# Making float32 weights from double-precision words: VectorE's last three steps replaced by one rounding pass and an integer add on GpSimd

## Chip, core and metric

The kernel runs on one core of a Trainium2 chip. The metric is the device time of one execution in microseconds. Times shown are medians over runs of the same kernel.

The engines are named as in the profile: PE is TensorE, DVE is VectorE, ACT is ScalarE, POOL is GpSimd, and SP is SyncE, which only issues DMAs here. PEld is PE's loading of stationary operands.

## What is computed

A recurrence over 768 time steps (RWKV-7) for 4 batches of 8 heads with head dimension 40, and after it an MLP with a sigmoid-gated activation on the 3072 rows of 320 channels that come out.

```python
state = zeros((B, H, D, D))
for t in range(S):
    y[:, :, t] = einsum('bhd,bhde->bhe', r_t, state)
    Sa = einsum('bhde,bhe->bhd', state, a_t)
    state = state * w_t[:, :, None, :] - einsum('bhd,bhe->bhde', Sa, b_t)
    state = state + einsum('bhd,bhe->bhde', v_t, k_t)
x = y.transpose(0, 2, 1, 3).reshape(B * S, H * D)
h = x @ w_in                                   # 320 -> 2048
out = (h * (1 / (1 + exp(-1.702 * h)))) @ w_out  # 2048 -> 320
```

The two weight matrices arrive as 64-bit floating-point numbers. The kernel works in float32, so it has to turn each 64-bit number into a 32-bit one on the chip.

## The kernel before

**The recurrence in chunks.** The 768 steps are cut into 12 chunks of 64, and the batches into two pairs, so there are 24 units; unit `i` is chunk `i // 2`, pair `i % 2`. Within a unit the steps are solved together by matmuls on PE: sums of logarithms of the decay (`ps_cum`, `ps_cumc`), scores (`ps_N`, `ps_A`, `ps_RV`), the inverse of a triangular matrix in five levels (`ps_level`, then `ps_Q`, `ps_T`), and then the part that depends on the state of the chunk before (`zr`, `ps_zT`, `ps_rz`, `ps_B`, `ps_X`, `ps_y`). Only this last part runs in order from chunk to chunk. Between the matmuls DVE, ACT and POOL copy, mask and scale: L686 and L665 are DVE's transposes between two levels, L747 and L714 copies of a level's result, L787 and L861 DVE's steps before `ps_X` and `ps_y`, L583, L588 and L591 scalings on POOL or DVE, L907 the scaling of the output `x`. L545 to L556 on ACT are the exponentials of a unit (L542 loads their table), L492 and L493 the logarithms for a later unit.

**The MLP.** When both pairs of a chunk are through, `x` goes to DRAM and comes back transposed (L917, L921), and the MLP of the chunk runs: four groups of 40 matmuls `ps_up` (L275 is the helper that issues every matmul), each followed by the gated activation on ACT (L942), and two groups of 64 matmuls `ps_down`, which add up over all four activations, with a copy (L966), an add (L968) and a store. Four pairs of PSUM banks are shared by all matmul groups. The MLP's matmuls are also what PE does while the recurrence waits.

**The weights.** `w_in` and `w_out` are each cut into four pieces of 128 x 1280 numbers; the pieces 0 to 3 are `w_in`, 4 to 7 `w_out`. A piece is loaded as pairs of 32-bit words (`raw`) into one of five places: two halves of a tile `extra`, two stretches of the final tile `w_sb` that later pieces will fill, and a part of `xT_all`. Each place is used again only when the piece before it is done. Five tasks then make 1280 float32 numbers of each piece in `w_sb`:

- `rebased` (L422, ACT): high word, read as float32, with its exponent brought near to that of the result
- `bounded` (L426, DVE): limits it
- `exponent` (L430 and L431, DVE): a shift by three bits and a mask writes the power of two alone over the high word in `raw`; a second shift makes the result without its last three bits in `w_sb`
- `fraction` (L434, DVE): the low word, as an unsigned number, times 2^-52 and times that power of two
- `joined` (L438, DVE): the sum of the two as float32

**Who sets the order.** Nothing is left to a scheduler at run time. `Plan.add` records each task with a rank, the engines that can do it with an estimated duration for each, and what it reads and writes. `Plan.order` then walks through time on these estimates and gives each engine, when it is free, the task of lowest rank that is ready. `paced` does this four times with shifted release times for the MLP and keeps the best order. The tasks marked `sbuf` on DVE and all tasks on POOL also share one modelled resource. The result is one fixed instruction order for each engine; an engine that waits holds up everything behind it. So other durations or other tasks for the weights can change the order on every engine, also of work that they have nothing to do with. The ACT table loads are put in after that, wherever the next function needs another table than the one loaded; the plan's durations include one for the exponentials and one for the logarithms of the later units, and none for the activation L942.

Ranks of the eight pieces are 14, 16, 20, 24, 35, 37, 39 and 41, where unit `i` has ranks around `10 * i`; so the weights are made while the first four or so units run.

Of the kernel before, what the change touches and what calls it, by code (L numbers as in the profile page):

```python
# [18 lines left out]
FP32 = mybir.dt.float32  # L19
INT32 = mybir.dt.int32  # L20
UINT32 = mybir.dt.uint32
INT64 = mybir.dt.int64
ALU = mybir.AluOpType
# [202 lines left out]
def rwkv7_gelu_quick(ctx: ExitStack, tc: tile.TileContext, time_d, v_d, w_d, wc_d, ak_d, b_d, rv_d, w_in, w_out, out):  # L226
    nc = tc.nc
# [5 lines left out]
    PIECE = w_in.shape[2]  # L233
# [21 lines left out]
    plan = Plan(dict(logw=3, wc=3, G=1, wch=3, wz=2, time=2, ak=2, b=2, rv=2, FT=3, GT=1, kh=2, bh=2, zr=2, rz=2,  # L255
                     A=1, B=1, RV=2, E0=2, W0=2, P21=2, PT=2, W=2, E=2, ES=2, EX=2, T=2, Tc=1, QT=1, zraw=2, zT=1, M=2, x=1, xT=3, g=4, ob=1), 4)
# [31 lines left out]
    def act(n):  # L288
        return {"ACT": 210.0 + 0.76 * n}
# [116 lines left out]
    def weight(n, rank, src):  # L406
        at = raws[n]
        def raw():
            if at == "x":
                return xT_all[:, 1:].rearrange("p s n -> p (s n)").bitcast(INT64)  # L410
            tile, k = spots[at]
            return tile[:, k * PIECE:(k + 2) * PIECE].bitcast(INT64)

        scale = lambda: w_sb[:, n * PIECE:(n + 1) * PIECE].bitcast(INT32)

        before = [("weight", m) for m in range(n) if raws[m] == at]
        there = [("weight", m) for m in range(n) if raws[m] in (f"w{n}", f"w{n - 1}")]
        word = lambda dt, w: raw().bitcast(dt).rearrange("p (n two) -> p n two", two=2)[:, :, w]

        def rebased(t):  # L420

            nc.scalar.activation(scale().bitcast(FP32), word(FP32, 1), ACT.Prelu, scale=2.0 ** -112, alpha=2.0 ** 32)  # L422

        def bounded(t):

            nc.vector.tensor_scalar(scale().bitcast(FP32), scale().bitcast(FP32), least, most, ALU.max, ALU.min)  # L426

        def exponent(t):

            nc.vector.tensor_scalar(word(INT32, 1), scale(), 3, -2 ** 23, ALU.logical_shift_left, ALU.bitwise_and)  # L430
            nc.vector.tensor_single_scalar(scale(), scale(), 3, op=ALU.logical_shift_left)  # L431

        def fraction(t):
            nc.vector.scalar_tensor_tensor(word(FP32, 1), in0=word(UINT32, 0), scalar=2.0 ** -52, in1=word(FP32, 1),  # L434
                                           op0=ALU.mult, op1=ALU.mult)

        def joined(t):
            nc.vector.tensor_add(scale().bitcast(FP32), scale().bitcast(FP32), word(FP32, 1))  # L438

        one, two = 170.0 + 0.48 * PIECE, 150.0 + 1.05 * PIECE  # L440
        T = lambda *names: [(name, n) for name in names]
        plan.add(rank, {"SP": 350.0}, lambda t: nc.sync.dma_start(raw(), src), reads=before, writes=T("wt"), size=128 * PIECE * 8)
        plan.add(rank, act(PIECE), rebased, reads=T("wt") + there, writes=T("rebased"))
        plan.add(rank, {"DVE": one, "sbuf": True}, bounded, reads=T("rebased"), writes=T("bounded"))
        plan.add(rank, {"DVE": 2 * one, "sbuf": True}, exponent, reads=T("bounded"), writes=T("exponent"))
        plan.add(rank, {"DVE": two, "sbuf": True}, fraction, reads=T("exponent"), writes=T("fraction"))
        plan.add(rank, {"DVE": two, "sbuf": True}, joined, reads=T("fraction"), writes=T("weight"))

    def weights():
        for n in range(len(raws)):  # L450
            weight(n, RANKS[n], w_in[n] if n < NQ else w_out[n - NQ])
# [636 lines left out]
```

## Times and profile before

| | |
|---|---|
| median of 3 runs | 723.49 us (722.95 to 725.37) |
| the profiled execution | 728.5 us |
| its span, first to last instruction | 726.7 us |
| mean granted clock of PE | 0.978 |
| PE busy | 677.6 us, 93% |
| PEld busy | 572.5 us, 79% |
| DVE busy | 430.0 us, 59% |
| ACT busy | 356.8 us, 49% |
| POOL busy | 187.9 us, 26% |
| DMA, all queues | 69.82 MB, mean 96 GB/s |

The page also cuts the span into 40 slices of 18 us; a digit is the busy share in tenths, 9 being 90% or more.

```
PE   4566997999999999999999999999999989999997
DVE  6578888956667666666756655666755556431000
ACT  4455655557554554554545465455457446446342120
POOL 8104143432431331330350320431530310200000
PEclk9879998999999999999999999999999999999999
```

Matmuls overlap in PE, so a busy PE is not PE at its peak. PEclk is the share of the full clock that PE was granted[...]. A line of a group of instructions reads: source line, engine, operation, output and inputs, shapes, count, then busy us, mean ns of one, and the idle time of the engine just before them with what ended it. A timeline line begins with start and duration in us.

### The profile page before, as it was taken

To read this page: it belongs to the slowest core of one execution; us is meant where nothing else is said; L and a number is where in the kernel's file an instruction comes from. 1 tells how busy PE (TensorE), PEld (TensorE's weight loads), DVE (VectorE), ACT (ScalarE), POOL (GpSimd) and SP (SyncE) were. 2 spreads that over 40 slices of the span, in tenths; PEclk is the share of its full clock that TensorE was granted. 3 is DMA by queue.
4 is the path that set the end of the run, shared out by engine and by line. 5 is a ranking of instruction groups with operands and counts; after the bars stand their busy time and mean duration, and the time that the engine had idled before them with its cause. 6 is when DMAs were issued, how large, how long until landed. Compare 5 with 4: busy or idle time off the path is not lost.

```text
span 726.7 us, 43527 instructions
## 1 busy us (share of the span) xinstructions
PE 677.6 (93%) x20256; PEld 572.5 (79%) x20256; DVE 430.0 (59%) x739; ACT 356.8 (49%) x705; POOL 187.9 (26%) x260
## 2 busy tenths in 40 slices
PE   4566997999999999999999999999999989999997
PEld 4555885799788789888888878887889978897564
DVE  6578888956667666666756655755666556431000
ACT  4455655557554554545465455457446446342120
POOL 8104143432431331330350320431530310200000
PEclk9879998999999999999999999999999999999999
DMA  7963542332251341351450440441340230110000
GB/s 216 351 251 93 165 124 86 107 96 78 91 145 55 109 120 49 88 158 32 119 136 22 116 130 31 119 118 39 120 112 23 85 95 5 40 49 30 18 5 20
DMA packets 31861, 69.82 MB, mean 96 GB/s; under 512 B 5056, under 2 KB 14272, under 8 KB 30656
## 3 DMA queue, kind: packets, MB, share of 16 engines
q1 hardware_dynamic: 31680, 67.03, 30.5%
q8 instruction: 159, 2.61, 1.4%
q14 instruction: 22, 0.18, 0.1%
HBM read 59.15 MB, written 7.86 MB: 92 GB/s over the span
## 4 chain that ended last, share of the span: by engine, by line
PE 83%; DVE 5%; issue 3%; ACT 3%; DMA 3%; POOL 2%; SPq 1%; POOLq 0%; DVEq 0%; ACTq 0%
PE ps_down L275 28%; PE ps_up L275 26%; PE ps_level L275 8%; PE ps_y L275 5%; PE ps_B L275 4%; PE ps_X L275 2%; DMA ak<-in_ak 2%; PE ps_Q L275 2%; PE ps_N L275 1%; PE ps_T L275 1%; PE ps_rz L275 1%; PE ps_A L275 1%; PE ps_RV L275 1%; PE ps_zT L275 1%; PE ps_cum L275 1%
## 5 line engine op out<-in xcount | busy, mean ns | idle before, releaser
L275 PE MATMUL ps_up<-xT_all,w_sb 64*64 64x256 f32 x3840 | 249.1, 378 | 2.6 <-ACT g L942 1.5
L275 PE MATMUL ps_down<-w_sb,g 64*64 64x320 f32 x3072 | 244.4, 434 | 3.1 <-DVE w_sb L438 2.5
L275 PEld LDWEIGHTS ps_up<-xT_all,w_sb 64*64 64x64 f32 x3840 | 160.6, 133 | 26.7 <-ACT g L942 1.8
L275 PEld LDWEIGHTS ps_down<-w_sb,g 64*64 64x64 f32 x3072 | 136.2, 134 | 45.3 <-issue 3.1
L670 ACT ACTIVATE EX<-ES,quads 128x256 f32<-128x256 f32 x116 | 52.6, 501 | 49.7 <-DVE ES L665 49.3
L591 POOL TENSOR_TENSOR kh<-time,G 128x320 f32<-128x320 f32 x24 | 22.0, 918 | 185.3 <-PE ps_y L275 91.4
L942 ACT ACTIVATE g<-ps_up 128x1024 f32<-128x1024 f32 x48 | 49.1, 1023 | 40.4 <-PE ps_up L275 40.1
L275 PEld LDWEIGHTS ps_level<-W,EX 64*64 64x64 f32 x2560 | 57.3, 134 | 7.4 <-ACT EX L670 1.4
L716 DVE TENSOR_TENSOR E<-two,ps_level 128x256 f32<-128x256 f32 x80 | 33.2, 415 | 40.3 <-ACT W L714 39.8
L275 PE MATMUL ps_level<-W,EX 64*64 64x64 f32 (+1 forms) x2560 | 55.7, 218 | 0.7 <-ACT EX L670 0.3
L714 ACT COPY W<-ps_level 128x512 f32<-128x512 f32 x51 | 29.8, 585 | 44.0 <-PE ps_level L275 43.9
L275 PE MATMUL ps_level<-PT,EX 64*64 64x64 f32 (+2 forms) x1280 | 36.6, 251 | 11.4 <-DVE EX L686 7.2
L968 DVE TENSOR_TENSOR ob<-ob,ps_down 128x320 f32<-128x320 f32 x24 | 11.6, 484 | 59.4 <-ACT ob L966 59.1
L275 PEld LDWEIGHTS ps_level<-PT,EX 64*64 64x64 f32 x1280 | 34.3, 152 | 15.2 <-DVE EX L686 7.0
L907 POOL TENSOR_TENSOR x<-zr,FT 128x128 f32<-128x128 f32 x84 | 42.8, 539 | 10.4 <-ACT zr L899 10.2
L583 POOL TENSOR_TENSOR ak<-ak,FT 128x512 f32<-128x512 f32 x21 | 27.3, 1299 | 53.2 <-DMA ak<-in_ak 26.2
L845 ACT COPY B<-ps_B 128x416 f32<-128x416 f32 x36 | 18.2, 506 | 44.1 <-PE ps_B L275 43.6
L275 PE MATMUL ps_y<-RV,kh 64*64 64x104 f32 x768 | 36.4, 252 | 2.3 <-DVE M L861 2.2
L665 DVE STREAM_TRANSPOSE ES<-E 128x256 f32<-128x256 f32 x80 | 35.6, 445 | 3.9
L275 PE MATMUL ps_y<-M,bh 64*64 64x104 f32 x768 | 36.5, 252 | 1.3 <-issue 1.3
L275 PEld LDWEIGHTS ps_y<-RV,kh 64*64 64x64 f32 x768 | 30.1, 134 | 6.4 <-DVE M L861 2.4
L861 DVE TENSOR_TENSOR M<-ps_X,later 128x832 f32<-128x832 f32 x24 | 24.5, 1021 | 17.6 <-PE ps_X L275 17.6
(140 smaller groups left out, 1132.9 us busy)
## 6 DMA issues: line engine op xcount, KB each, us to landing
ak<-in_ak SPq DMA_DIRECT2D x48, 160.0 KB
time<-in_time SPq DMA_DIRECT2D x24, 320.0 KB
rv<-in_rv SPq DMA_DIRECT2D x48, 160.0 KB
xT_all<-x_dram SPq DMA_DIRECT2D x48, 160.0 KB
wc<-in_wc SPq DMA_DIRECT2D x20, 264.0 KB
logw<-in_w SPq DMA_DIRECT2D x24, 160.0 KB
b<-in_b SPq DMA_DIRECT2D x48, 80.0 KB
RV<-in_v SPq DMA_DIRECT2D x24, 160.0 KB
```

What stands on the lines that cost most here:

```text
L275: nc.tensor.matmul(o, lhsT, rhs, start=start, stop=True, skip_group_check=True)
L583: plan.add(R, {"DVE": 690.0, "POOL": 1270.0, "sbuf": True}, lambda t: of(t.engine).tensor_mul(ahT(), ahT(), FT_of(i)), reads=T("ak", "FT") ...
L591: plan.add(R + 4, {"POOL": 870.0, "DVE": 490.0, "sbuf": True}, lambda t, n=n, dst=dst: of(t.engine).tensor_mul(dst(i)[:, :, :D], by_head(t ...
L665: plan.add(rank, dve(256), lambda t: nc.vector.transpose(ES(n), source(t)), writes=[key("ES", n, 6)], **reads)
L670: nc.scalar.activation(dst[:, :, h], ES(n), ACT.Copy, scale=quads[:, h, :1])
L714: plan.add(rank, any2(512), lambda t: copy(t.engine)(tiles_of(W(n + 1)), blocks(psum(t, ""), 64)), writes=[key("W", n + 1, 5)], pair=pair)
L716: plan.add(rank, dve(256), lambda t: nc.vector.tensor_sub(tiles_of(E(n + 1)), every(two32, [128, 2, 4, 32]), blocks(psum(t, ""), 64)[:, :, ...
L845: plan.add(R, any2(416), lambda t: copy(t.engine)(dst(), psum(t, "")[:, :, :208]), writes=[("Bv", i)] if x and c > 0 else T("B"), pair=(na ...
L861: plan.add(R + 1, dve(832), lambda t: nc.vector.tensor_tensor(M_of(i).rearrange("p (j b) n -> p b j n", b=2), psum(t, "")[:, :, :416].rear ...
L907: of(t.engine).tensor_mul(x[:, b ^ u, b], both(i)[:, at, :64], FT_of(i)[:, at])
L942: plan.add(-45, act(1024), lambda t: nc.scalar.activation(g_of(c * NQ + q).rearrange("p m r n -> p r m n"), psum(t, "").rearrange("p r (m ...
L968: plan.add(-45, dve(320), lambda t: nc.vector.tensor_add(ob_of(serial), ob_of(serial), psum(t, "")[:, 1, :DM]), reads=[("ob", serial)], wr ...
```

## The change

The power of two is not made any more. The high word is still shifted by three bits (`shifted`, L430 now), which leaves three zero bits at its low end. The low word times 2^-29 is rounded to an integer from 0 to 8 and written over the high word in `raw` (`rounded`, L434): that many units of the last place are missing. As the high word is no longer needed once L422 has read it, this pass waits for L422 alone. POOL then adds the two as 32-bit integers (`joined`, L438), so that a carry runs on into the exponent by itself. The DVE passes of a piece go from five to three, and POOL gets one instruction for each piece. The estimates for the plan change with it.

```diff
-        def exponent(t):
-
-            nc.vector.tensor_scalar(word(INT32, 1), scale(), 3, -2 ** 23, ALU.logical_shift_left, ALU.bitwise_and)
+        def shifted(t):
+
             nc.vector.tensor_single_scalar(scale(), scale(), 3, op=ALU.logical_shift_left)
 
-        def fraction(t):
-            nc.vector.scalar_tensor_tensor(word(FP32, 1), in0=word(UINT32, 0), scalar=2.0 ** -52, in1=word(FP32, 1),
-                                           op0=ALU.mult, op1=ALU.mult)
+        def rounded(t):
+
+            nc.vector.tensor_single_scalar(word(INT32, 1), word(UINT32, 0), 2.0 ** -29, op=ALU.mult)
 
         def joined(t):
-            nc.vector.tensor_add(scale().bitcast(FP32), scale().bitcast(FP32), word(FP32, 1))
-
-        one, two = 170.0 + 0.48 * PIECE, 150.0 + 1.05 * PIECE
+
+            nc.gpsimd.tensor_tensor(out=scale(), in0=scale(), in1=word(INT32, 1), op=ALU.add)
+
+        one, add = 170.0 + 0.52 * PIECE, 200.0 + 2.1 * PIECE
...
         plan.add(rank, {"DVE": one, "sbuf": True}, bounded, reads=T("rebased"), writes=T("bounded"))
-        plan.add(rank, {"DVE": 2 * one, "sbuf": True}, exponent, reads=T("bounded"), writes=T("exponent"))
-        plan.add(rank, {"DVE": two, "sbuf": True}, fraction, reads=T("exponent"), writes=T("fraction"))
-        plan.add(rank, {"DVE": two, "sbuf": True}, joined, reads=T("fraction"), writes=T("weight"))
+        plan.add(rank, {"DVE": one, "sbuf": True}, shifted, reads=T("bounded"), writes=T("parts"))
+        plan.add(rank, {"DVE": one, "sbuf": True}, rounded, reads=T("rebased"), writes=T("parts"))
+        plan.add(rank, {"POOL": add}, joined, reads=T("parts"), writes=T("weight"))
```

`PIECE` is 1280. In both kernels the instructions on SP are the same in number, 390, and so are all matmuls. The order of both kernels' instructions can be read off the built programs: in it the number of table loads on ACT is 38 before and 59 after.

## The prediction

> **What bounds the kernel now.** I read four views in this order: busy time by stretch, the waits of PE, the timeline of DVE, POOL and PE in the worst stretch, and the rows of the lines that the diff touches. The columns of the first view are stretch and length, then busy us (instructions) of PE, PEld, DVE, ACT and POOL, granted clock, DMA share, GB/s.
>
> ```profile
> 25.00:50.00 25.00, 16.24 (x442) 14.17 (x435) 17.73 (x24) 14.73 (x30) 1.48 (x2) 0.70 0.94 324
> 50.00:75.00 25.00, 16.18 (x653) 14.80 (x656) 21.43 (x27) 13.26 (x30) 9.55 (x11) 0.92 0.30 87
> 75.00:100.00 25.00, 24.37 (x721) 21.70 (x717) 20.28 (x26) 16.72 (x30) 9.49 (x9) 0.95 0.47 147
> 100.00:125.00 25.00, 19.98 (x508) 15.60 (x504) 21.85 (x26) 12.29 (x24) 5.89 (x5) 0.87 0.35 112
> 300.00:400.00 100.00, 98.63 (x3081) 85.38 (x3073) 63.43 (x114) 53.91 (x108) 29.02 (x37) 1.00 0.34 98
> ...
> 114.00:120.00 6.00, 1.62 (x48) 1.09 (x52) 5.93 (x8) 4.15 (x10) 3.14 (x3) 0.88 0.10 30
> 120.00:126.00 6.00, 6.00 (x144) 3.96 (x136) 3.12 (x4) 1.41 (x4) 0.37 (x1) 0.55 0.00 0
> ```
>
> From 150 us on PE is busy 98 to 100% of the time, and the program's last 55 us are nothing but MLP matmuls, so whatever idle time of PE goes away earlier should come off the end. Idle PE time is 8.8 + 8.8 + 0.6 + 5.0 = 23.2 us from 25 to 125 us, and that is where all eight weight pieces are made from their double-precision words: L426 first runs at 26.0 us, L438 last at 128.8 us. DVE is 81 to 87% busy from 50 to 125 us. The worst place:
>
> ```profile
> 113.33 2.33 DVE L434 SCALAR_TENSOR_TENSOR extra<-extra 128x1280 f32<-128x1280 uint32 x1
> 115.58 0.70 DVE L686 STREAM_TRANSPOSE EX<-ps_level 128x512 f32<-128x512 f32 x1
> ...
> 117.50 1.74 DVE L438 TENSOR_TENSOR w_sb<-w_sb,extra 128x1280 f32<-128x1280 f32 x1
> ```
>
> ```profile
> 113.03 1.28 POOL L588 TENSOR_TENSOR ak<-ak,GT 128x512 f32<-128x512 f32 x1
> ```
>
> ```profile
> 99.71 2.38 PE L275 MATMUL ps_down<-w_sb,g 64*64 64x320 f32 x32
> ...
> 116.34 0.67 PE L275 MATMUL ps_level<-PT,EX 64*64 64x32 f32 x32 [2.35 <-DVE EX L686]
> ...
> 119.30 4.54 PE L275 MATMUL ps_down<-w_sb,g 64*64 64x320 f32 x32 [2.04 <-DVE w_sb L438]
> ```
>
> L434 of piece 6 lasts 2.33 us (1.53 when alone), since POOL's L588 is still running when it starts. The transpose behind it in DVE's queue comes 2 us late, and PE waits for it. Then PE waits for the piece itself. After this pause the clock is 0.55, and 32 matmuls take 4.54 us that took 2.38 at 99.7 us. The place costs 4.4 idle (114 to 120 us), 2.2 on these matmuls, and 0.8 on the next two groups (1.02 and 1.10 us where 0.64 is usual): 7.4 us.
>
> **What the Trainium skill says.** "SBUF — State Buffer", Who interferes with whom: a VectorE instruction in a 2-port mode, or with two SBUF inputs beside a GpSimd instruction that reads SBUF, excludes GpSimd for the whole instruction, and the later one waits. The trace agrees: L434, 1.53 us alone, takes 2.59 us at 91.67 us beside L588 (91.16, 1.72 us). "VectorE: DVE Perf Modes", Mode 2×_2P: one source and destination in SBUF give two elements a cycle for 4-byte types; the trace's L431 agrees (0.83 us for 1280 elements, against 1.53 for the two-input L434). "GPSIMD Engine Reference", Exact integer add: an add with both inputs and the output of one 32-bit integer type is done natively; the trace of before has no integer operation on POOL.
>
> **The change, part by part.** Rows: mean ns follow the busy us.
>
> ```profile
> L434 DVE SCALAR_TENSOR_TENSOR extra<-extra 128x1280 f32<-128x1280 uint32 x5 | 9.0, 1804 | 0.0
> L431 DVE TENSOR_SCALAR w_sb<-w_sb 128x1280 int32<-128x1280 int32 x8 | 7.2, 895 | 0.3
> L438 DVE TENSOR_TENSOR w_sb<-w_sb,extra 128x1280 f32<-128x1280 f32 x5 | 7.6, 1527 | 0.1
> L583 POOL TENSOR_TENSOR ak<-ak,FT 128x512 f32<-128x512 f32 x21 | 27.3, 1299 | 53.2 <-DMA ak<-in_ak 26.2 <-ACT FT L545 18.5 <-PE ps_level L275 3.9
> ```
>
> Removed from DVE (the forms not shown here included): eight L430, 4.4 + 1.7 + 0.8 = 6.9 us; eight L434, 9.0 + 3.1 + 2.6 = 14.7; eight L438, 7.6 + 2.9 + 1.5 = 12.0. Together 33.6 us. Kept: L426, and L431's shift. Added to DVE: eight roundings, one source, strided on both sides. L430 has a strided output and still takes 0.82 to 0.88, so I take 0.83 each, 6.6 us; if the stride on both sides drops it to the rate of L434 it is 1.53, 12.2 us. DVE loses 27 us (21 at worst), nearly all between 26 and 129 us.
>
> Added to POOL: eight adds of 128x1280. From L907 (128 elements, 539 ns) and L583 (512, 1299) an element costs 1.98 ns, so 1.30 + 768 × 0.00198 = 2.8 us; with the slope from L591 (320, 905) it is 2.9. I take 2.85, in all 23 us. The integer type could make it cheaper (2 us) or dearer (4 us); no row shows it. POOL had 26 us of work from 24 to 132 us, so it has room. But each add holds the ports that DVE's passes need. In the changed program's order piece 1's rounding is followed at once by piece 2's two passes, so the second of these can stand behind piece 1's add for 2.85 us, with L787 and L861 of the recurrence behind it.
>
> Moved: the plan recomputes every engine's order, and this is no small part. SP keeps its 390 instructions and PE its matmuls. On ACT the table loads go from 38 to 59: the exponential of G (L556) and the logarithms (L492) now stand behind a gelu in seven groups, instead of directly behind the channel exponentials, and each time the table is switched back. The trace of before has one such group:
>
> ```profile
> 486.87 1.28 ACT L942 ACT_TABLE_LOAD   x1
> ...
> 489.99 1.28 ACT L556 ACT_TABLE_LOAD   x1
> ...
> 491.74 1.28 ACT L492 ACT_TABLE_LOAD   x1
> ```
>
> There ACT is 4.94 and 4.96 us busy in two stretches of 5 us, and PE waits 1.11 us for the gelu at 489.2 us.
>
> The sum. (a) The stall at 114 to 126 us: piece 6 needs one short pass less before the transposes, L434's successor is half as long, and in the new order 40 matmuls of the fourth ps_up group (4.3 us) are still left as filler there. Against that, piece 6's add stands behind L583 and L588 on POOL and is 1.3 us longer than L438 was. I take 5 of the 7.4 us; bounds 0 and 7.4. (b) From 25 to 75 us: by the waits of PE, it waits for DVE's transposes, T, M and zT for 7.2 − 2.35 (counted in (a)) + 1.1 + 2.2 + 1.4 = 9.6 us. Three pieces are made there, each with 33.6 / 8 − 0.83 = 3.4 us less of DVE. Of these 10 us some 4.4 stand ahead of such a wait in DVE's queue, and the lock gives 2.85 back: −1.5, bounds −5 and +3. (c) The table loads: 21 × 1.28 = 26.9 us on ACT, which is 49% busy overall. Six more split groups at 1.1 us are 6.7; filler will cover about half: +3, bounds 0 and 10.8 (40% of the 26.9). Sum: −5 − 1.5 + 3 = −3.5 us. The profiled execution took 728.5 us (span 726.7), so it would take 725.0; the median shown is 723.5, the same saving gives 720.0.
>
> **Rivals.** *Nothing comes out* (723.0): the stall at 114 us shrinks by 3 to 5 us, and table loads and the lock take that back. For it: ACT also carries 1.4 us of L422 per piece and the copies that PE waits for. Against it: DVE, not ACT, ended PE's waits before 150 us.
>
> *The table loads decide* (slower, 729.0): place, ACT from 85 us on; price, 26.9 us, of which 40% reaches PE, 10.8 − 5.3 of the gain left = +5.5. It decides from 6.5 us on, 24% of the added loads. For it: three of the seven groups fall between 80 and 125 us, where gelus, L422 and level copies share ACT, and the one observed group cost PE 1.1 us. Against it: ACT was half idle, and a gelu has two PSUM pairs of slack.
>
> *The shared ports decide* (slower, 726.5): eight adds of 2.85 us block DVE's passes, and half of that, 11 us, delays the recurrence; as PE has no filler before 78 us, two such blocks (5.7 us) outweigh what (b) brings, and (a) recovers only half. For it: both engines together keep almost the former load on these ports (33.6 us gone, 6.6 + 23 added). Against it: DVE's PSUM reads pass beside an add.
>
> **How the numbers follow.** Forecast (faster) 0.43, own range 715.5 to 721; no change 0.22; table loads 0.25; shared ports 0.10. A measurement of this kernel tells 0.3%, about 2.2 us, from no change. So faster 0.43, same 0.22, slower 0.35. The low end, 715.0, takes (a) whole with (c) near nothing; the high end, 729.5, takes in the second rival's centre. Beyond both ends I leave 0.17.
>
> **What would show it.** DVE busy falls from 430 to about 404 us and POOL's rises from 188 to about 211; the rounding at L434 takes 0.83 us, L438 on POOL 2.85; 59 table loads; between 110 and 130 us PE idles under 2 us and its clock stays at 1.00; PE's waits for w_sb from POOL stay below 1 us. I am wrong if PE's idle time before 150 us stays near 37 us, if an add takes over 4 us, or if PE's wait for g (L942), 1.8 us in all, grows past 7 us.

## The result and the profile after

The changed kernel is slower: 727.12 us median of 16 runs (722.67 to 732.84), against 723.04 us for the kernel before in runs on the same chip. The ratio is 1.0074, 95% interval 1.0051 to 1.0096, so 0.7% or some 5 us. The profiled execution took 730.79 us, its span 729.1 us.

The view of busy time by stretch, kernel after; columns as before (stretch and length, busy us and instructions of PE, PEld, DVE, ACT, POOL, then granted clock, DMA share, GB/s):

```profile
25.00:50.00 25.00, 16.81 (x455) 15.64 (x458) 13.85 (x21) 12.14 (x28) 4.38 (x3) 0.66 0.88 314
50.00:75.00 25.00, 18.30 (x737) 17.05 (x731) 18.65 (x29) 15.72 (x38) 14.81 (x12) 0.86 0.29 85
75.00:100.00 25.00, 22.86 (x677) 19.85 (x671) 21.23 (x30) 18.32 (x27) 15.93 (x13) 1.00 0.55 177
100.00:125.00 25.00, 22.67 (x740) 18.85 (x736) 18.39 (x33) 16.97 (x25) 13.01 (x8) 1.00 0.32 109
114.00:120.00 6.00, 5.65 (x232) 5.32 (x228) 5.54 (x11) 3.04 (x7) 2.96 (x2) 1.00 0.12 40
120.00:126.00 6.00, 5.62 (x208) 4.57 (x204) 5.83 (x10) 2.40 (x6) 3.21 (x4) 1.00 0.36 108
250.00:300.00 50.00, 46.53 (x1400) 35.97 (x1395) 32.70 (x64) 29.98 (x51) 10.57 (x16) 0.97 0.33 93
300.00:350.00 50.00, 50.00 (x1532) 40.95 (x1528) 28.05 (x54) 25.49 (x48) 9.00 (x11) 1.00 0.28 82
350.00:400.00 50.00, 47.65 (x1381) 37.09 (x1373) 28.20 (x51) 28.51 (x49) 18.89 (x22) 0.97 0.31 91
400.00:450.00 50.00, 47.16 (x1500) 39.54 (x1504) 30.66 (x60) 28.42 (x50) 17.79 (x23) 1.00 0.35 100
```

The kernel before, from 250 to 450 us:

```profile
250.00:350.00 100.00, 99.14 (x3146) 88.78 (x3142) 63.34 (x118) 54.34 (x104) 27.07 (x32) 1.00 0.31 90
350.00:450.00 100.00, 97.73 (x3034) 80.16 (x3027) 62.15 (x110) 53.37 (x109) 30.00 (x40) 1.00 0.34 97
```

The stall at 114 us is gone: PE is busy 5.65 and 5.62 of 6 us, at full clock, where it had 1.62 of 6 and then a clock of 0.55. PE's idle time before 150 us falls from 36.9 to 30.4 us. But from 250 to 450 us, where the kernel before idles 3.1 us, PE now idles 8.7 us, and the clock dips to 0.97 twice.

Idle time alone doesn't tell what a lower clock costs, so I also counted the matmuls done. In the timeline's full stretches a `ps_up` starts every 54 ns, a `ps_down` every 67 ns and another matmul every 19 ns on average. With these as weights, every matmul recorded up to a time makes an amount of work; the lag is the time minus that work. Only differences between kernels count.

| lag in us at | 150 us | 250 us | 350 us | 450 us | 650 us |
|---|---|---|---|---|---|
| before | 58.0 | 54.7 | 53.0 | 52.0 | 50.8 |
| after | 49.4 | 48.3 | 50.9 | 57.0 | 53.5 |

At 150 us the changed kernel is 8.6 us ahead. At 450 us it is 5.0 us behind: it has fallen back by 7.6 us, and the kernel before has made up 6.0. So the gain came, and was given back and more between 250 and 450 us, long after the last weight piece.

A part of that loss belongs to this one execution. At 252 us PE waits for the x that comes back from DRAM. Timeline of SP, then a row of PE's waits from 250 to 450 us (us in total, times, longest), kernel after:

```profile
245.45 0.69 SPq L917 DMA_DIRECT2D x_dram<-x  x2
249.69 1.11 SPq L921 DMA_DIRECT2D xT_all<-x_dram  x2
```

```profile
PE ps_up L275 <- DMA xT_all<-x_dram: 2.1, 1, 2.1
```

The load of x is issued 4.2 us after its store, which SP waits for. In e3, e5, e7 and e17 (experiments below), where PE's order is the same up to there, the same load comes 2.7 to 3.0 us after its store, and PE waits only 0.6 us at this place. Here the clock is 0.56 from 254 to 257 us, and the lag grows by about 5 us from 250 to 275 us, against 2 in e7. The execution is also 3.7 us slower than the median. So some 3 us of the lag after 250 us are its own; the rest has to be found elsewhere.

The groups of the new steps in the kernel after (busy us, mean ns of one, idle before), each form apart, first VectorE's, then GpSimd's, then the table loads:

```profile
L430 DVE TENSOR_SCALAR w_sb<-w_sb 128x1280 int32<-128x1280 int32 x8 | 9.7, 1207 | 0.2
L434 DVE TENSOR_SCALAR extra<-extra 128x1280 int32<-128x1280 uint32 x5 | 4.9, 985 | 0.0
L434 DVE TENSOR_SCALAR w_sb<-w_sb 128x1280 int32<-128x1280 uint32 x2 | 1.6, 784 | 0.0
```

```profile
L438 POOL TENSOR_TENSOR w_sb<-w_sb,extra 128x1280 int32<-128x1280 int32 x5 | 15.5, 3103 | 12.7 <-DVE extra L434 12.7
L438 POOL TENSOR_TENSOR w_sb<-w_sb 128x1280 int32<-128x1280 int32 x2 | 6.4, 3200 | 5.9 <-DVE w_sb L434 5.9
```

```profile
L942 ACT ACT_TABLE_LOAD x24 | 30.8, 1283 | 0.4
L556 ACT ACT_TABLE_LOAD x7 | 9.0, 1283 | 0.1
L492 ACT ACT_TABLE_LOAD x7 | 9.0, 1283 | 0.1
```

The rounding runs at the short rate (784 ns when undisturbed), the integer add takes 3.0 to 3.2 us, and the loads are 59, as counted. VectorE is busy 414.6 us, GpSimd 210.0 us, ACT 376.7 us.

ACT holds PE up in two places between 350 and 450 us. This is the first. Timeline of ACT, kernel after (start, duration, instruction, idle before it and its releaser):

```profile
383.17 1.28 ACT L542 ACT_TABLE_LOAD   x1
...
385.84 1.28 ACT L942 ACT_TABLE_LOAD   x1
387.13 1.02 ACT L942 ACTIVATE g<-ps_up 128x1024 f32<-128x1024 f32 x1
388.05 0.58 ACT L714 COPY W<-ps_level 128x512 f32<-128x512 f32 x1
388.65 1.28 ACT L556 ACT_TABLE_LOAD   x1
389.94 0.44 ACT L556 ACTIVATE G<-ps_cum 128x320 f32<-128x320 f32 x1
390.40 1.28 ACT L492 ACT_TABLE_LOAD   x1
```

And PE at the same time:

```profile
388.21 1.09 PE L275 MATMUL ps_up<-xT_all,w_sb 64*64 64x256 f32 x16 [0.62 <-ACT g L942]
390.44 0.81 PE L275 MATMUL ps_RV<-rv 64*64 64x64 f32 x32 [1.13 <-ACT G L556]
391.01 1.09 PE L275 MATMUL ps_N<-b,ak 64*64 64x64 f32 x32
391.86 1.95 PE L275 MATMUL ps_up<-xT_all,w_sb 64*64 64x256 f32 x16
...
400.68 0.69 PE L275 MATMUL ps_rz<-rv,zT 64*64 64x64 f32 x32 [1.10 <-ACT g L942]
```

From 383 to 391.7 us ACT does four table loads. PE waits 0.62 us for the activation between two of them, 1.13 us for the exponential of G behind the third, and 1.10 us for the next activation, which needs a fifth load. After the second wait 16 matmuls `ps_up` take 1.95 us where 1.04 us is usual, and the clock is 0.50 from 391 to 394 us. Not every such pause costs clock: after the 1.10 us at 400 us it stays at 1.00. At 442 us the same tables are switched once more and PE waits 1.3 us for G, again at a clock of 1.00. By the waits of PE, summed over its rows from 150 us on, it waits 6.8 us for ACT; in the kernel before it was 1.5 us.

### The profile page after: what moved, and what is told of

Its sections match the earlier page's. It is cut to its first block, busy times and chain, and to the rows that moved or that the text cites. A ratio compares the mean times of both kernels' runs of the same rounds, so it can differ in the third digit from the quotient of the medians.

```text
span 729.1 us, 43555 instructions
## 1 busy us (share of the span) xinstructions
PE 681.7 (94%) x20256; PEld 556.1 (76%) x20256; DVE 414.6 (57%) x754; ACT 376.7 (52%) x698; POOL 210.0 (29%) x268
## 4 chain that ended last, share of the span: by engine, by line
PE 81%; ACT 9%; DVE 4%; DMA 3%; issue 3%; POOL 0%; SPq 0%; DVEq 0%; ACTq 0%; POOLq 0%
PE ps_up L275 26%; PE ps_down L275 25%; PE ps_level L275 9%; PE ps_y L275 4%; PE ps_B L275 4%; PE ps_X L275 2%; ACT L942 2%; PE ps_N L275 2%; PE ps_T L275 1%; PE ps_Q L275 1%; ACT g L942 1%; PE ps_RV L275 1%; PE ps_A L275 1%; PE ps_zT L275 1%; PE ps_rz L275 1%
## 5 line engine op out<-in xcount | busy, mean ns | idle before, releaser
L275 PE MATMUL ps_up<-xT_all,w_sb 64*64 64x256 f32 x3840 | 255.2, 381 | 6.8 <-DMA xT_all<-x_dram 2.3
L275 PE MATMUL ps_down<-w_sb,g 64*64 64x320 f32 x3072 | 239.0, 431 | 0.2 <-DVE zr L897 0.2
L275 PEld LDWEIGHTS ps_up<-xT_all,w_sb 64*64 64x64 f32 x3840 | 155.5, 134 | 39.0 <-issue 6.4
L275 PEld LDWEIGHTS ps_down<-w_sb,g 64*64 64x64 f32 x3072 | 126.4, 133 | 46.9 <-PE ps_level L275 0.3
L670 ACT ACTIVATE EX<-ES,quads 128x256 f32<-128x256 f32 x126 | 57.1, 500 | 49.4 <-DVE ES L665 47.1
L942 ACT ACTIVATE g<-ps_up 128x1024 f32<-128x1024 f32 x48 | 49.1, 1024 | 32.4 <-PE ps_up L275 31.9
L714 ACT COPY W<-ps_level 128x512 f32<-128x512 f32 x56 | 32.8, 585 | 52.1 <-PE ps_level L275 52.0
L275 PE MATMUL ps_level<-W,EX 64*64 64x64 f32 (+1 forms) x2560 | 55.7, 218 | 1.5 <-DVE A L602 1.3
L583 POOL TENSOR_TENSOR ak<-ak,FT 128x512 f32<-128x512 f32 x21 | 29.0, 1381 | 58.2 <-DMA ak<-in_ak 38.2
L907 POOL TENSOR_TENSOR x<-zr,FT 128x128 f32<-128x128 f32 x80 | 40.1, 530 | 5.5 <-ACT zr L899 2.8
L660 POOL TENSOR_TENSOR PT<-two,PT 128x256 f32<-128x256 f32 x19 | 13.8, 729 | 82.0 <-DVE PT L653 66.0
L966 ACT COPY ob<-ps_down 128x320 f32<-128x320 f32 x18 | 7.7, 425 | 52.4 <-PE ps_down L275 52.3
```

Of the source, the lines that this page charges most:

```text
L275: nc.tensor.matmul(o, lhsT, rhs, start=start, stop=True, skip_group_check=True)
L583: plan.add(R, {"DVE": 690.0, "POOL": 1270.0, "sbuf": True}, lambda t: of(t.engine).tensor_mul(ahT(), ahT(), FT_of(i)), reads=T("ak", "FT") ...
L660: plan.add(R, {"DVE": 430.0, "POOL": 750.0, "sbuf": True}, lambda t: of(t.engine).tensor_sub(at(W0_t, i)[:, :, :32], two32.unsqueeze(1).to ...
L670: nc.scalar.activation(dst[:, :, h], ES(n), ACT.Copy, scale=quads[:, h, :1])
L714: plan.add(rank, any2(512), lambda t: copy(t.engine)(tiles_of(W(n + 1)), blocks(psum(t, ""), 64)), writes=[key("W", n + 1, 5)], pair=pair)
L907: of(t.engine).tensor_mul(x[:, b ^ u, b], both(i)[:, at, :64], FT_of(i)[:, at])
```

## The experiments

Each was timed in five rounds beside the kernel before on one chip; the ratio and its 95% interval are to that kernel before, so compare ratios and not times. "New steps" are the rounding and the add on GpSimd, "old steps" the mask, fraction and float add on VectorE. The theories in the first expectations are: 1, the new steps help and the added table loads cost more; 2, any other order than that of the kernel before loses; 3, the adds on GpSimd hold up VectorE.

| run | steps | order dealt for | time us | ratio |
|---|---|---|---|---|
| e1_old_order_new_ops | new | before | 725.15 | 1.0017 (0.9993 to 1.0041) |
| e2_new_order_old_ops | old | after, 59 loads | 743.09 | 1.0263 (1.0229 to 1.0297) |
| e3_regrouped | new | after, 47 loads | 729.34 | 1.0079 (1.0050 to 1.0108) |
| e4_other_estimate | new | 0.48, 38 loads | 719.36 | 0.9948 (0.9925 to 0.9971) |
| e5_whole_groups | new | after, 38 loads | 729.55 | 1.0068 (1.0048 to 1.0087) |
| e6_sooner_x | new | e5, x sooner | 730.99 | 1.0071 (1.0040 to 1.0101) |
| e7_short_add | new, short add | after | 729.91 | 1.0055 (1.0036 to 1.0074) |
| e8_before_redealt | old | 0.50, 50 loads | 741.48 | 1.0232 (1.0200 to 1.0265) |
| e9_later_order_210 | new | after to 210 us | 726.51 | 1.0038 (1.0018 to 1.0058) |
| e10_later_order_253 | new | after to 253 us | 726.37 | 1.0039 (1.0022 to 1.0057) |
| e11_before_redealt_46 | old | 0.46, 41 loads | 728.71 | 1.0069 (1.0046 to 1.0091) |
| e12_after_redealt_46 | new | 0.46, 39 loads | 727.23 | 1.0048 (1.0024 to 1.0071) |
| e13_good_order_old_ops | old | e4 | 730.04 | 1.0061 (1.0038 to 1.0085) |
| e14_more_table_loads | new | e4, 56 loads | 735.94 | 1.0140 (1.0101 to 1.0179) |
| e15_old_order_short_add | new, short add | before | 721.43 | 0.9942 (0.9912 to 0.9972) |
| e16_after_redealt_60 | new | 0.60, 39 loads | 733.37 | 1.0102 (1.0071 to 1.0133) |
| e17_after_one_table | new | after, 21 loads | 720.91 | 0.9935 (0.9916 to 0.9955) |
| e18_good_order_one_table | new | e4, 21 loads | 719.08 | 0.9923 (0.9893 to 0.9953) |

**Steps and order apart.** In the first run the plan of the kernel before stays, with its estimates, and the tasks issue the new steps; in the second the plan of the kernel after stays, and the tasks issue the old ones (the same edit the other way round, with the mask and the fraction in one task). The diff is the first one's.

```diff
         def exponent(t):
-            nc.vector.tensor_scalar(word(INT32, 1), scale(), 3, -2 ** 23, ALU.logical_shift_left, ALU.bitwise_and)
             nc.vector.tensor_single_scalar(scale(), scale(), 3, op=ALU.logical_shift_left)
         def fraction(t):
-            nc.vector.scalar_tensor_tensor(word(FP32, 1), in0=word(UINT32, 0), scalar=2.0 ** -52, in1=word(FP32, 1),
-                                           op0=ALU.mult, op1=ALU.mult)
+            nc.vector.tensor_single_scalar(word(INT32, 1), word(UINT32, 0), 2.0 ** -29, op=ALU.mult)
         def joined(t):
-            nc.vector.tensor_add(scale().bitcast(FP32), scale().bitcast(FP32), word(FP32, 1))
+            nc.gpsimd.tensor_tensor(out=scale(), in0=scale(), in1=word(INT32, 1), op=ALU.add)
```

> The plan is that of the kernel before, with its tasks, estimates and 38 table loads; only what three tasks issue is that of the changed kernel: no power of two, the rounding pass, and the add on POOL at the place in time where DVE's add stood. Theory 1 (the new operations help, the table loads that the new order adds cost more): PE's idle time before 150 us falls from 37 to about 31 us, nothing is lost later, 718 us against 723. Theory 2 (any other order than the one of before loses, whatever the loads): also about 718, since the order is the old one. Theory 3 (POOL's adds hold the ports and delay DVE): no gain, 726 or more.

> The plan is that of the changed kernel, with 59 table loads; the tasks issue what the kernel before issued: two shifts' worth of DVE passes, the product and the sum, all on DVE, nothing on POOL. Theories 1 and 2: the loss of the new order without the gain of the new operations, 730 to 734 us. Theory 3: without the adds on POOL it is back at 723, plus at most 2 us.

The new steps gain nothing in the old order, where theories 1 and 2 expected 5 us, and the old steps lose 2.6% in the new one, more than any of the theories expected. So steps and order belong together. What happens in the old order shows at its stall. Timeline of GpSimd and then of PE, first experiment:

```profile
113.12 0.72 POOL L658 TENSOR_TENSOR PT<-two,PT 128x256 f32<-128x256 f32 x1 [2.21 <-DVE PT L651]
113.79 2.94 POOL L436 TENSOR_TENSOR w_sb<-w_sb,extra 128x1280 int32<-128x1280 int32 x1
```

```profile
112.77 0.43 PE L275 MATMUL ps_level<-PT,ident 64*64 64x128 f32 x8
116.78 4.54 PE L275 MATMUL ps_down<-w_sb,g 64*64 64x320 f32 x32 [3.59 <-POOL w_sb L436]
```

The float add of piece 6 that PE waited for has become an integer add on GpSimd behind L658. PE waits 3.59 us for it and then runs 32 matmuls in 4.54 us, as before. The stall stays, with another engine at its end.

**The adds.** Both runs do the add for 128 of 1280 numbers, e7 in the order of the kernel after, e15 in that of the kernel before.

```diff
-            nc.gpsimd.tensor_tensor(out=scale(), in0=scale(), in1=word(INT32, 1), op=ALU.add)
+            nc.gpsimd.tensor_tensor(out=scale()[:, :128], in0=scale()[:, :128], in1=word(INT32, 1)[:, :128], op=ALU.add)
```

> The changed kernel in its own order, with the add on GpSimd done for the first 128 of the 1280 numbers of each piece only; the other numbers keep their low bits unadded, so this part of the computation is left out. It takes 22 us off GpSimd, and with it every hold of the shared ports by the adds. Theory 3 (the adds make the changed kernel slow, by blocking VectorE's passes or by finishing the weights late): 4 us or more less, 723 or under. Theories 1 and 2: 0 to 2 us less, 725 to 727.

> The first experiment (the order of the kernel before, new steps, 725 us) with the add on GpSimd done for 128 of 1280 numbers only; the other low bits stay unadded, so this part of the computation is left out. If the adds, which in that order stand late on GpSimd behind other work, take back what VectorE gains: PE's waits for GpSimd before 150 us fall from 9.9 us to 4 or less and the time to 719 to 722. If the order simply leaves no use for a faster VectorE: within 1.5 us of 725.

In the old order the adds cost 0.75% (1.0017 to 0.9942), or 5.4 us: PE's waits for GpSimd before 150 us fall from 9.9 to 4.9 us, and at the stall it waits 1.09 us for the short add in place of 3.59. In the order dealt for them they cost 0.2%, within the intervals. So they explain why the old order gains nothing, and not why the changed kernel is slower.

**Other deals.** Only the estimate of a one-source pass differs, for new steps (e4, e12, e16) or old ones (e8, e11).

```diff
-        one, add = 170.0 + 0.52 * PIECE, 200.0 + 2.1 * PIECE
+        one, add = 170.0 + 0.48 * PIECE, 200.0 + 2.1 * PIECE
```

> The changed kernel with one number changed: the plan's estimate for a short DVE pass is 170 + 0.48 per element as in the kernel before, instead of 0.52 (784 instead of 836 ns). The instructions are the same, the order is dealt anew and has 38 table loads. Theory 1: the gain before 150 us stays and the later loss is gone, about 718 us. Theory 2: another order than the one of before, so again a loss, 725 or more. Theory 3: the adds are still there, 726 or more.

> The kernel before with all its own steps; only the estimate of a one-source pass on VectorE in the plan goes from 170 + 0.48 to 170 + 0.50 ns an element, so that all engines get another order (50 table loads in place of 38). Theory 2 (the order of the kernel before was a lucky one for its steps, and another estimate spoils it whatever the steps): 730 or more. If the re-dealt order alone does nothing systematic: 720 to 727. Theory 1: 12 more loads in split groups cost 3 to 5 us, 727 to 728.

> The kernel before with all its own steps; only the estimate of a one-source pass in the plan goes from 170 + 0.48 to 170 + 0.46 ns an element (41 table loads). A second sample of how far the order alone moves the old steps, with nearly as few table loads as before. If the order alone scatters the time by 1 to 2 per cent, and the order of before was a good one: 727 to 740. If the first re-dealt run was slow because of its 50 table loads: 722 to 726.

> The changed kernel's steps; only the estimate of a one-source pass goes from 170 + 0.52 to 170 + 0.46 ns an element (39 table loads). A third order for the new steps, beside the changed kernel (727) and the run with 0.48 (719). If the new steps gain under most orders: 716 to 724. If 0.48 was a lucky order: 725 to 735.

> The changed kernel's steps; only the estimate of a one-source pass goes from 170 + 0.52 to 170 + 0.60 ns an element (39 table loads). A further order for the new steps, beside 0.46 (727), 0.48 (719) and 0.52 (727). If the order alone scatters the time by about 1%, anything from 717 to 733 is possible and says only how wide the scatter is; if fewer table loads made the good run good, 717 to 722.

The same new steps give 0.9948, 1.0048, 1.0074 (the changed kernel) and 1.0102; the same old steps 1.0000, 1.0069 and 1.0232. The order alone moves the time by 1.5% with the new steps and by 2.3% with the old, and the number of loads alone doesn't sort the deals: e12 and e16, with 39 loads, have lags of 55.7 and 60.4 us at 150 us and so hardly a lead to lose. e4 has 38 loads and a lag of 49.9 us at 150 us, like the changed kernel, and 47.6 us at 450 us: it keeps 4.4 of its lead of 8.1 us. It beats both kernels, but it is the only one of four deals for the new steps that does; by what was expected of e12 it was a lucky one.

**The steps in the good order.** e13 has the order of e4 and the old steps, by the edit of the second experiment.

> The order of the run with the other estimate (0.48, 719 us), instruction for instruction on PE, ACT, SP and nearly so on the others; only the steps of the weights are the old ones, on VectorE: the two shifts, the fraction and the float add. The same as the second experiment, for the order that came out fastest. If the new steps bring the gain and an order fits only the steps it was dealt for: 728 to 740. If that order is simply a good one, for old steps too: 719 to 724.

The steps bring 1.1% there (1.0061 to 0.9948), and the lag at 150 us is 60.3 with the old, 49.9 with the new steps. The gain is real in an order dealt for the new steps. In the order dealt for the old ones they bring nothing (e1), or 0.6% once most of the add is left out (e15).

**Whole groups, and the pause for x.** In e3 an activation between the exponentials, G and the logarithms is moved behind them where no other task forbids it (47 loads left); in e5 the rest is made whole too, by moving G and the logarithms ahead of it. The diff is a part of that of e5.

```diff
+                    if not any(g in t.after or clash(g, t) for t in later):
+                        out.remove(g)
+                        out.insert(out.index(b) + 1, g)
...
+                    elif not any(t in b.after or clash(b, t) for t in sooner):
+                        out.remove(b)
+                        out.insert(out.index(g), b)
...
-    for t in tasks:
+    for t in regroup(tasks):
```

> The changed kernel; after its plan is made, the activation that stands between a unit's channel exponentials, its G and the logarithms is put behind them on ACT where nothing in between needs it. Table loads fall from 59 to 47, all else keeps its order. Theory 1: about half of the 21 added loads go, so about half of the later loss does: 722 us against 727 of the changed kernel, waits of PE for G (L556) below 1 us. Theories 2 and 3: no change beyond 1 us, 727.

> The changed kernel's order on every engine, but in all seven split groups the gated activation no longer stands between the channel exponentials, the exponential of G and the logarithms: it is moved behind them, or, where PE needs it sooner, G and the logarithms are moved ahead of it. Table loads 59 to 38, as in the kernel before. Theory 1 (the split groups cost the changed kernel what its new steps gain): the two groups that the first regrouping left split, at 383 to 398 and at 437 to 446 us, hold 4.1 us of PE's waits and are followed by a lower clock, so these go now: 5 to 8 us less than the changed kernel, about 720. Theory 2 (the order of the rest costs it, the groups don't): within 2 us of the first regrouping, 727 to 730. Theory 3 (the adds on GpSimd): no difference, 727 to 729.

In e6, which starts from e5, PE also issues the level and the `ps_y` that lead to the late x at 252 us ahead of three `ps_down`, and SP the store of that x ahead of two loads.

> The same as the run with whole groups, and in addition the matmuls ps_y of the eighth unit, whose result becomes the x that PE waits for at 252 us, are issued on PE ahead of three groups of ps_down, and SP issues the store of that x ahead of two loads. Nothing else changes its place. If the lead of the changed kernel is also lost because its MLP is ahead of the recurrence and runs out of work before x is back, the 2.1 us wait of ps_up for xT_all at 252 us shrinks to under 0.6 us, the clock between 250 and 275 us rises from 0.93 to 1.00, and the time is 2 to 3.5 us under that of the run with whole groups. If such a pause is only taken later, it is the same within 1 us.

e3 and e5 miss what theory 1 expected of them, with 1.0079 and 1.0068, and e6, with 1.0071, is no faster than e5. Why is seen at the same place as above. Timeline of ACT, then of PE, in e5:

```profile
386.89 0.46 ACT L493 ACTIVATE logw<-logw 128x320 f32<-128x320 f32 x1
387.36 1.28 ACT L945 ACT_TABLE_LOAD   x1
388.66 1.02 ACT L945 ACTIVATE g<-ps_up 128x1024 f32<-128x1024 f32 x1
```

```profile
386.64 1.26 PE L275 MATMUL ps_down<-w_sb,g 64*64 64x320 f32 x16
389.73 1.09 PE L275 MATMUL ps_up<-xT_all,w_sb 64*64 64x256 f32 x16 [1.83 <-ACT g L945]
```

The wait for G is gone, and the wait for the activation grows from 0.62 to 1.83 us, since the activation now stands behind G, the logarithms and its own load. At this place PE needs both at once; sorting them by table only chooses which is late. By the waits of PE from 150 us on, e5 still waits 5.0 us for ACT, where the changed kernel waits 6.8. e6 was to take away the pause for x at 252 us, but in e5, from which it starts, PE waits only 0.6 us there: e6 had nothing to gain and doesn't tell what a late x costs. I took these three runs for the end of theory 1, wrongly, as the last runs show.

**Another later order.** Estimates of tasks from the tenth unit on are changed, so that PE's order is the same until 210 or 253 us and another after that.

```diff
-            plan.add(R, {"ACT": 1600.0 + (1300.0 if i >= EARLY else 0.0)}, exp_channel, reads=T("cum", "sums"), uses=T("wc"),
+            plan.add(R, {"ACT": 1600.0 + (1300.0 if i >= EARLY else 0.0) + (200.0 if i >= 9 else 0.0)}, exp_channel, reads=T("cum", "sums"), uses=T("wc"),
```

> The changed kernel with one estimate in the plan changed: the channel exponentials count 200 ns more from the tenth unit on. PE's order is the same as in the changed kernel for its first 2840 instructions, until about 210 us, with all eight weight pieces and the whole lead of 8 us that they bring; after that all engines get another order (46 table loads). Theory 4 (the early gain is real, and the order after 150 us that the plan happens to deal gives it back): another later order is not bound to give it back; time 717 to 722. Theory 5 (the lead can't be kept, since the recurrence sets the pace and the MLP only runs ahead of it): the same as the changed kernel within 2 us, 726 to 729, with PE's idle time after 150 us near 17 us again.

> As the run before, with 150 ns in place of 200: PE's order is that of the changed kernel for 3496 instructions, until about 253 us, so that the pause of 2 us at 252 us for x is kept, and the order after it is another one (46 table loads). Theory 4: the pause and its lower clock stay, 3 to 4 us; the rest of the loss, 5 us between 350 and 450 us, may go: 720 to 724. Theory 5: 726 to 729.

Both come out between the two theories, 1.0038 and 1.0039, or 726 us for a kernel before of 723, nearer to theory 5. The pause that e10 was to keep is not in its trace. The lag of e9 is 51.4 us at 450 us, where the changed kernel has 57.0 and the kernel before 52.0. So another later order loses less, but this one keeps only 0.6 us of the lead.

**Table switching itself.** e14 takes the good order of e4 and adds 18 loads, in five units, with no activation moved.

```diff
+            if i in MORE:
+                nc.scalar.preload_act_table_set("gelu_apprx_sigmoid_and_others")
             nc.scalar.activation(G_of(i), psum(t, "")[:, :, :160], ACT.Exp, scale=-1.0)
...
+            if i - 2 in MORE:
+                nc.scalar.preload_act_table_set("gelu_apprx_sigmoid_and_others")
             if i >= BY_PE:
                 nc.scalar.activation(wc_of(i), wc_of(i), ACT.Ln)
```

> The run with the other estimate (0.48, 719 us, 38 table loads), its order unchanged, with 18 table loads added: in five units the table of the gated activation is loaded between the channel exponentials and the exponential of G, and again ahead of the logarithms, and the right one is loaded anew. 18 x 1.28 = 23 us more on ACT, no other change. Theory 1 (table loads in these groups cost PE what the prediction priced for the rival, 40%): 9 us more, 728. As the prediction had it in its forecast (1.1 us a group, half of it covered): 3 us more, 722. If filler covers them: within 1 us of 719.

The ratio goes from 0.9948 to 1.0140: 1.9%, or 13.9 us for 23.1 us of loads, 60%, more than theory 1 expected. The lag goes from 51.4 us at 150 us to 61.8 at 450 us, a rise as in the changed kernel.

e17 and e18 take the switching away instead, in the order of the kernel after and in that of e4. They put an exponential in place of the MLP's gated activation, so that function is left out, and of the table loads 21 remain.

```diff
-                ACT.Gelu_apprx_sigmoid), writes=[("g", c * NQ + q)], pair=("up", c * NQ + q))
+                ACT.Exp, scale=2.0 ** -6), writes=[("g", c * NQ + q)], pair=("up", c * NQ + q))
```

> The changed kernel, order unchanged on every engine, with an exponential in place of the MLP's gated activation (so this function is left out): all functions on ACT then lie in one table, and of 59 loads the 21 explicit ones ahead of the channel exponentials and at the start remain. 38 loads, 49 us, less on ACT. If table switching costs the changed kernel its lead: PE's waits for ACT after 150 us, 6.8 us, fall under 2, and the time to 712 to 718, within 2 us of the other order under the same edit. If the order loses it elsewhere (x, VectorE, the order on PE): 723 to 726, and 5 us or more above the other order.

> The run with the other estimate (0.48, 719 us), order unchanged, with the same edit: an exponential in place of the gated activation, 21 loads in place of 38. Its PE hardly waits for ACT after 150 us (0.5 us), so in both theories 715 to 719. It is the yardstick for the run before.

The order of the kernel after falls from 1.0074 to 0.9935, that of e4 only from 0.9948 to 0.9923, and the two are then the same within their intervals. An activation lasts 1022 to 1024 ns in both, as before, so nothing but the loads has gone from ACT. Busy time by stretch in e17:

```profile
250.00:300.00 50.00, 49.02 (x1440) 38.45 (x1439) 32.80 (x64) 25.84 (x51) 12.15 (x16) 1.00 0.35 97
300.00:350.00 50.00, 49.65 (x1540) 45.61 (x1544) 28.04 (x55) 21.52 (x43) 10.13 (x15) 1.00 0.27 77
350.00:400.00 50.00, 48.54 (x1507) 39.19 (x1501) 30.49 (x58) 25.50 (x51) 16.87 (x18) 1.00 0.31 88
400.00:450.00 50.00, 48.36 (x1551) 42.60 (x1547) 32.57 (x65) 24.92 (x49) 17.71 (x23) 1.00 0.34 98
```

PE's idle time from 250 to 450 us is 4.4 us instead of 8.7 (2.1 of which were the late x), the clock stays at 1.00, and its waits for ACT after 150 us are 0.7 us instead of 6.8. The lag is 46.8 us at 150 us and 44.7 at 450 us: of a lead of 11.2 us over the kernel before, 7.3 stay.

So the switching between tables is what makes the order of the kernel after slower than that of e4. That it costs more there because PE needs an activation and a unit's exponentials at once is read from the traces at 383 us in the kernel after and in e5; no run changes this alone. The price of the 21 added loads follows from the two pairs: 1.39% minus 0.25% is 1.14%, about 8.3 us of 724 (the intervals combined as independent give 3.5 us either way), 31% of their 26.9 us. It is an upper figure if the 17 loads that e4 has too cost more in the other order; that was not told apart. And it is a price against the order of e4: the kernel before, which has 38 loads too, was not run with one table.

## Why the prediction was wrong

- *Durations.* Rounding 0.78 us undisturbed (0.83 taken), add 3.0 to 3.2 us by its groups (2.85 taken, 2 to 4 as bounds), POOL 210.0 us (211), 59 loads. VectorE has 414.6 us, not 404: L430 waits for an add (9.7 us for eight where the shift took 7.2), and VectorE has 754 instructions instead of 739, although each piece has two fewer: the new plan gives it work that ACT or GpSimd did (twenty more copies at L757, five more at L845), which the sum had left out.
- *(a) The stall.* Right, and more than taken: from 110 to 130 us PE idles 0.96 us instead of 5.59, and the clock is 1.00. The order and the steps both have a part in it. The new order with the old steps (e2) idles 3.81 us there, at a clock of 1.00; the new steps in the old order (e1) idle 6.81 us at 0.83, at the end of an add.
- *(b) 25 to 75 us.* Right: idle time falls by 2.7 us (1.5 taken). The lock of piece 1's add on piece 2's shift is there, just as read from the order. Timeline of GpSimd, then of VectorE, kernel after:

```profile
56.24 3.44 POOL L438 TENSOR_TENSOR w_sb<-w_sb 128x1280 int32<-128x1280 int32 x1 [3.44 <-DVE w_sb L434]
```

```profile
56.08 0.81 DVE L426 TENSOR_SCALAR w_sb<-w_sb 128x1280 f32<-128x1280 f32 x1
56.93 3.44 DVE L430 TENSOR_SCALAR w_sb<-w_sb 128x1280 int32<-128x1280 int32 x1
60.29 0.47 DVE L787 SCALAR_TENSOR_TENSOR T<-ps_T,quads,T 128x256 f32<-128x256 f32 x1
```

  The shift starts 0.7 us after the add and ends 0.7 us after it, so it waits for the add and then takes its own time. L787 stands behind it, and by the waits of PE `ps_X` then waits 3.5 us for its T, once. This agrees with what the prediction quoted of the Trainium skill, "SBUF — State Buffer", Who interferes with whom.
- Together (a) and (b) were to bring 6.5 us, and PE's idle time before 150 us fell by 6.5 us. That these agree is luck: the two places brought 4.6 and 2.7 us, the other stretches with a gain 2.3, and 75 to 110 us, which the sum left out, lost 3.1. Of these, 1.6 are a wait for G at 105 us, behind a table load of one of the split groups.
- *(c) The table loads: the step that failed.* "Six more split groups at 1.1 us are 6.7; filler will cover about half: +3". The last runs show about 8 us, against the order of e4. The mechanism was there, and the rival that had it decide, with 40% of 26.9 us and 729.0 us, was the right case. With 8.3 us in place of 3 the sum is +1.8 us; 5 us were measured, and the 3 us between are within the uncertainty of that figure. The price was taken from one group, 1.1 us of PE's wait, and halved. What it left out: several PE waits belong to one group (0.62, 1.13 and 1.10 us above), the lower clock after some of the pauses, and that the MLP is no filler there, because the `ps_up` next in PE's queue waits itself for the activation that is late. ACT's mean of 49% said nothing about such a place.
- *The signs.* None of the three signs of being wrong came: PE's idle time before 150 us fell, no add took over 3.44 us, and PE's wait for g grew from 1.8 to 3.3 us only. The last was the wrong sign to name: ACT's other results count as well, above all G (3.0 us after 150 us). All waits for ACT after 150 us, 1.5 to 6.8 us, would have shown it.
- *The other rivals.* "The shared ports decide" falls: the short add changes the time by 0.2%. "Nothing comes out" had the gain at the stall taken back by the table loads, as it was, but no loss beyond that.

What stays open: whether a plan that knows the table on ACT and charges each switch would deal such an order by itself. That was not tried on the chip. And e5 shows that the number of loads is not the whole of it: with the same 38 loads as e4 the order stays slow; its trace shows the clash on ACT still there.

## What to carry to other kernels

Where a planner deals the order, a local saving is worth what the newly dealt order leaves of it: here the same steps gave 0.9948 to 1.0102, so time several deals before judging the steps, and try the new steps in the old order and the old steps in the new one. Before you explain a pause in a trace, look for it in other executions of the same order: the one for x at 252 us was in one trace of five. Price a table load on ACT by what PE needs around it, not by ACT's mean load; between 31% and 60% of the added loads' time came out at the end. When a sum of early gains is right and the end is not, count work done over time: it shows where the lead goes.

## What the runs showed of the hardware

- An integer add of 128x1280 on GpSimd took 2.93 to 3.44 us. The float operations of the same engine had let the prediction expect 2.8 to 2.9 us, so the integer type is hardly dearer.
- A VectorE shift that started 0.7 us after such an add ended 0.7 us after it: 3.44 us instead of 0.8. A VectorE step that adds a PSUM tile to an SBUF tile (L848) took its usual 0.59 us inside another add, at 96.56 us.
- Rounding unsigned to signed integers with both sides strided still ran at the short rate, 784 ns for 1280 elements.
- Pauses of PE of 0.62 and 1.13 us within 3 us were followed by 3 us at a clock of 0.50 (16 `ps_up` in 1.95 us instead of 1.04), and one of 2.1 us at 252 us by 3 us at 0.56. Single pauses of 1.10 and 1.3 us in the same trace, and one of 1.83 us in e5, were followed by a clock of 1.00.
- A table load took 1.28 us in each of the 59 cases, and the function behind it started at once: the load at 388.65 us, G at 389.94 us.
